# Another written-out order for a one-core attention and gated projection kernel, with zero products in the early gaps, a first load in three pieces and a last block in two halves

## The chip, the cores and the metric

The kernel runs on one core of one Trainium2 chip. The time is the device time of one execution in microseconds (us); the profile's span is the part of a profiled execution that the instructions fill. Engines are named as in the profile: PE multiplies matrices (PEld is its weight load), DVE works on vectors, ACT evaluates functions, POOL is hardly used, SP issues most loads. SPq and ACTq are the queues from which DMAs are issued.

## The reference, cut to what matters

Eight batches, eight heads, 512 local and 32 global positions, head dimension 64. Global queries see all 544 keys; a local query sees the 32 global keys and the local keys at most 32 positions away.

```python
s_g = scale * np.matmul(q_g, k_all.transpose(0, 1, 3, 2))
out_g = np.matmul(sm(s_g), v_all)
mask = np.abs(pos[:, None] - pos[None, :]) <= window        # window = 32
s_ll = np.where(mask, scale * np.matmul(q_l, k_l.transpose(0, 1, 3, 2)), -1e9)
out_l = np.matmul(sm(np.concatenate([s_lg, s_ll], axis=-1)), np.concatenate([v_g, v_l], axis=2))
x = concatenate([out_g, out_l], axis=2)  ->  (B, 544, 512)
gate = sigmoid(causal convolution of x along the positions, 5 taps, one weight per channel)
out = (gate * (x @ w_val)) @ w_out
```

## The kernel before, in words

A **unit** u is two heads of one batch; there are 32, four to a batch b. One unit's local attention is a chain of tasks, each of which is a few instructions on one engine:

- s{u} (PE, L567): 32 small score products in a program row, 64 in the trace, 64x32 weights each;
- mx{u}.h (DVE, L579): adds the mask, scales, and takes the maximum, four instructions per half h with one read of the accumulator behind each;
- exp{u}.h (ACT, L586), t{u}.h (PE transposes, L592), tc{u}.h (a copy out of PSUM, ACT L404 or DVE L406);
- av{u} (PE, L603): 64 value products in the trace; den, rec (DVE); norm{u} (DVE, one instruction, or ACT, eight, L624); xt{u} (PE transposes, L632); xc{u} (copy).
- Then xh, xl split the result into two parts for the wide products, and tap, conv build the gate on DVE. For the first two units the convolution is done on PE (pc, L693) with diagonal matrices that ACT makes (dg, L682).

The global queries of a batch have their own chain (gs, gmax, gexp, gt, gtc, gav, gden, grec, gnorm, gx, gxc). The two weights arrive as 64-bit numbers and are turned into a high and a low 32-bit part on DVE and ACT (w{k}.s0 to s7 and w{k}.high). For each batch then follow g1 (PE, L717: three products of 512 columns for each of 16 pairs of tiles), the gate (gv, gh, gl), and g2 (PE, L739: the same for the output weight), a copy ob and a store st. The 256 global rows of all batches are done last under the key "g" (gxh, gxl, gconv, sigg, g1.g, g2.g, ob.g, st.g; tiles ghg, glg, obg).

**What sets the order.** A long string `ORDER` names every task once, in one line, with the engine where there is a choice ("tc1.0:DVE") and the PSUM bank ("s4@53"). Every engine gets its instructions in the order in which its tasks stand in that string. A planner (`Plan.order`) walks it, keeps count of buffers and banks, and estimates times; the estimates set no waits, but decide where `keep_clock` puts products of zeros (L803) into PE's line: in before wherever the estimated gap is over `KEEP` = 900 ns, up to the first g1. Loads on SP are issued in the order of the string and wait for the PE instruction that stands ahead of them there. The first 13 loads are issued at once: q0, mask, q1, w0, q2, v0, q3, w1, v1, w2, v2, w3, v3 (L416, L953), q{u} being queries and keys of a unit, v{u} its values.

The last store: ACT copies the first half of obg (L745), DVE copies the second half (L746), then four DMAs of 64 KB write it, two from SP and two from ACT (L939).

Of the kernel before, what the change touches and what calls it, by code (L numbers as in the profile page):

```python
# [19 lines left out]
KW = 5  # L20
# [30 lines left out]
cw s0@01 mx0.0 mx0.1 exp0.0 w0.s0 s1@23 mx1.0 exp0.1 exp1.0 w0.s1 t0.1@1 t0.0@0 mx1.1 exp1.1 tc0.0 w0.s2 w0.s3 tc0.1 dg0  # L51
w0.s4 t1.0@2 w0.s5 t1.1@3 w0.s6 tc1.0:DVE av0@0 w0.s7 den0 rec0 norm0 s2@24 mx2.0 xt0@5 w0.high dg1 xc0 w1.s0 gs0@06
halo0 pc0.0@5 w1.s1 exp2.0 t2.0@2 tc1.1 mx2.1 w1.s2 gmax0.0 pc0.1 xh0 w1.s3 gmax0.1 w1.s4 w2.s0 pc0.2 w1.s5 exp2.1 tc2.0
av1@6 w2.s1 den1 w1.s6 rec1 w2.s2 w1.high iq4 xl0 t2.1@4 gexp0.1 s3@23 gexp0.0 tc2.1 w2.s3 norm1:ACT gt0.0@0 w1.s7
gtc0.0 mx3.0 pc0.3 w2.high w3.s0:ACT xt1@4 mx3.1 pc0.4 xc1 w3.s1 wi4 w2.s4 av2@0 w3.s2 gav0.0@4 exp3.1 halo1 den2 w3.s3
gt0.1@2 exp3.0 gtc0.1 w2.s5 conv0.3 w3.s4 pc1.0@6 t3.1@7 w2.s6 t3.0@2 xh1 iq5 w3.s5 iq6 rec2 norm2:ACT gav0.1 tc3.0 iv4
w3.s6 w2.s7 iq7 w3.s7 xl1 tc3.1 s4@53 xt2@0 w4.s0:ACT gden0 mx4.0 pc1.1 grec0 w4.s1 gnorm0 w4.s2 mx4.1 pc1.2 gx0@7 w4.s3
xc2 av3@4 exp4.0 gxc0 fix0 den3 s5@73 exp4.1 w4.s4 t4.0@2 tap2:ACT xh2 t4.1@0 iv5 pc1.3 rec3 halo2:ACT mx5.0 pc1.4 xl2
tc4.0 g1.0.0.0@7 norm3:ACT tc4.1 conv2.0 w4.s5 conv2.1 xt3@2 av4@0 conv1.3 w4.s6 exp5.0 xc3 w4.high conv2.2 w4.s7 t5.0@6
g1.0.0.1 den4 tc5.0 conv2.3 xh3 g1.0.0.2 rec4 s6@62 tap3:ACT mx5.1 norm4 exp5.1 wi5 xl3 w3.high gs1@40 t5.1@3 mx6.0  # L60
g1.0.0.3 exp6.0 halo3:ACT tc5.1 mx6.1 xt4@6 gmax1.0 fix1 exp6.1 gexp1.0 wi6 iv7 conv3.0 t6.0@2 w5.s0:ACT av5@4
g1.0.1.0@3 gmax1.1 den5 conv3.1 g1.0.1.1 g1.0.1.2 xc4 iv6 tc6.0 g1.0.1.3 t6.1@2 rec5 g1.0.2.0@6 gexp1.1 g1.0.2.1 w5.s1
conv3.2 w5.s2 conv3.3 w6.s0:ACT w5.s3 sig0 w6.s1 w5.s4 w5.high g1.0.2.2 norm5 s7@01 w5.s5 sig1 gv.0.0 tc6.1 w6.s2 w5.s6
gv.0.1 gt1.0@4 iq8 w5.s7 sig2 gh.0.0 g1.0.2.3 mx7.0 gtc1.0 gl.0.0 wi7 iq9 g1.0.3.0@7 gh.0.1 g1.0.3.1 sig3 iq10 g1.0.3.2
av6@4 w6.s3 exp7.0 gav1.0@0 gv.0.2 den6 gt1.1@2 gtc1.1 mx7.1 rec6 w6.s4 gl.0.1 xt5@6 exp7.1 g1.0.3.3 g2.0.0.0@1 norm6
gv.0.3 w7.s0:ACT t7.0@4 tc7.0 t7.1@5 w6.s5 tc7.1 gav1.1 w7.s1 gh.0.2 av7@2 iv8 w6.s6 w7.s2 w6.s7 gden1 gl.0.2 gh.0.3
iq11 w7.s3 w6.high den7 xc5 xt6@5 g2.0.0.1 iv10 grec1 g2.0.0.2 w7.s4 rec7 w7.s5 xh5 norm7:ACT gnorm1 s8@46 iv9 s9@70
# [123 lines left out]
class Plan:  # L191
# [38 lines left out]
    def order(self):  # L230
# [8 lines left out]
        def put(t):  # L239
# [12 lines left out]
            if t.eng != "FREE":  # L252
                at = max(at, free[t.eng])
# [48 lines left out]
            if t.eng == "DMA" and t.name != "first":  # L302
                self.loads = self.loads[-15:] + [(max([t.start + BEGINS] + [b for _, b in self.loads[-1:]]), t.end + LANDS)]
# [731 lines left out]
```

## Time and profile before

| | us |
|---|---|
| median of 3 runs | 362.09 |
| the three runs | 360.68, 362.09, 363.57 |
| the profiled execution | 361.64 |
| its span | 359.9 |
| PE busy | 349.9 |
| DVE busy | 315.3 |
| ACT busy | 254.3 |

PE is busy nearly throughout: of the 40 equal slices of the span every one but the last is at 8 tenths or more, and most at 9 or more. ACT is at 9 tenths for most of the first quarter and falls off later. A matmul's end is modelled, and consecutive matmuls overlap in the record, so PE's pace is read from start to start. The granted PE clock is below 9 tenths of full speed in one slice only, the second, which runs from 9 to 18 us.

### The profile page before, as it was taken

The page shows a single profiled execution, that of the slowest core. Times are in us where ns is not written, and L with a number is a line of the kernel's source. Part 1 is how long each engine was busy: PE and PEld are TensorE (multiplying, and loading weights), DVE is VectorE, ACT ScalarE, POOL GpSimd, SP SyncE. Part 2 cuts the span into 40 slices and gives each one's busy share as a digit, 9 for nine tenths or more (in the row PEclk, how much of TensorE's full clock was granted, in tenths as well). Part 3 has the DMA queues.
Part 4 walks back from the last instruction along what each step waited for, and adds up shares of the span by engine and source line. Part 5 has one row for each costly group of instructions (what it writes and reads, how often), then busy time and mean ns, then how long its engine had stood idle before and what let it go on. Part 6 is the DMA issues. An engine that isn't in the chain of part 4 may idle for free.

```text
span 359.9 us, 14810 instructions
## 1 busy us (share of the span) xinstructions
PE 349.9 (97%) x6331; PEld 280.0 (78%) x6331; DVE 315.3 (88%) x1085; ACT 254.3 (71%) x652; POOL 0.8 (0%) x7
## 2 busy tenths in 40 slices
PE   8899999899999999999999999999999999999995
PEld 4666687778787888788878877888878888888894
DVE  4899999999989899899899997989599696988981
ACT  3899999897897688987788566776659458523131
POOL 0000000000000000000000000000000000000000
PEclk9899999999999999999999999999999999999999
DMA  7995947695675734925666482823854101000223
GB/s 280 400 362 166 359 156 279 209 402 193 226 235 199 276 104 108 391 102 171 221 241 237 159 277 104 262 67 132 283 165 173 62 2 51 13 29 36 112 87 87
DMA packets 17249, 66.73 MB, mean 185 GB/s; under 512 B 1952, under 2 KB 4000, under 8 KB 17184
## 3 DMA queue, kind: packets, MB, share of 16 engines
q1 hardware_dynamic: 12240, 57.12, 45.2%
q10 hardware_dynamic: 4944, 8.67, 6.6%
q8 instruction: 49, 0.80, 0.9%
q14 instruction: 16, 0.13, 0.1%
HBM read 56.87 MB, written 8.91 MB: 183 GB/s over the span
## 4 chain that ended last, share of the span: by engine, by line
PE 81%; ACT 8%; DMA 5%; DVE 3%; issue 1%; SPq 1%; ACTq 0%; DVEq 0%
PE psum L717 25%; PE psum L739 23%; PE psum L603 7%; PE psum L567 7%; PE psum L592 7%; PE psum L632 4%; DMA v<-in_vw_dram 3%; PE psum L531 3%; DMA out_dram<-ob 2%; ACT pm L586 2%; PE psum L493 2%; ACT xs L624 2%; PE psum L511 1%; DVE gate L668 1%; ACT xc L404 1%
## 5 line engine op out<-in xcount | busy, mean ns | idle before, releaser
L586 ACT ACTIVATE pm<-pm,mx 128x128 f32<-128x128 f32 x256 | 80.9, 407 | 25.8 <-DVE mx L579 22.5
L668 DVE SCALAR_TENSOR_TENSOR gate<-xc,cw,gate 128x512 f32<-128x512 f32 x120 | 87.7, 745 | 1.1 <-ACT gate L397 0.4
L579 DVE CUSTOM_DVE_ANT_0 pm<-psum,mask 128x128 f32<-128x128 f32 x256 | 57.4, 285 | 5.2 <-PE psum L567 5.2
L717 PE MATMUL psum<-xh,wvh 128*128 128x512 f32 x128 | 53.8, 421 | 0.0
L739 PE MATMUL psum<-woh,gh 128*128 128x512 f32 x128 | 53.0, 414 | 0.0
L717 PE MATMUL psum<-xl,wvh 128*128 128x512 f32 x128 | 50.6, 396 | 0.0
L717 PE MATMUL psum<-xh,wvl 128*128 128x512 f32 x128 | 50.5, 395 | 0.0
L739 PE MATMUL psum<-woh,gl 128*128 128x512 f32 x128 | 50.2, 392 | 0.0
L739 PE MATMUL psum<-wol,gh 128*128 128x512 f32 x128 | 50.0, 391 | 0.0
L404 ACT COPY pts<-psum 128x512 f32<-128x512 f32 x49 | 28.6, 601 | 16.0 <-PE psum L592 16.0
L592 PE MATMUL psum<-ident,pm 128*128 128x128 f32 x256 | 38.0, 278 | 0.6 <-ACT pm L586 0.3
L567 PE MATMUL psum<-qk 64*32 64x128 f32 x2048 | 38.1, 281 | 0.5 <-ACT pm L586 0.4
L603 PEld LDWEIGHTS psum<-v,pts 128*32 128x32 f32 x2048 | 31.1, 111 | 8.3 <-issue 4.7
L567 PEld LDWEIGHTS psum<-qk 64*32 64x32 f32 x2048 | 30.3, 108 | 8.5 <-issue 3.6
L592 PEld LDWEIGHTS psum<-ident,pm 128*128 128x128 f32 x256 | 29.6, 140 | 9.1 <-ACT pm L586 2.7
L603 PE MATMUL psum<-v,pts 128*32 128x65 f32 x2048 | 34.9, 224 | 1.4 <-DMA v<-in_vw_dram 1.2
L717 PEld LDWEIGHTS psum<-xh,wvl 128*128 128x128 f32 x128 | 24.0, 188 | 5.6 <-issue 0.2
L739 PEld LDWEIGHTS psum<-woh,gl 128*128 128x128 f32 x128 | 24.0, 188 | 5.3
L717 PEld LDWEIGHTS psum<-xh,wvh 128*128 128x128 f32 x128 | 24.3, 190 | 4.5 <-DVE xl L664 0.2
L717 PEld LDWEIGHTS psum<-xl,wvh 128*128 128x128 f32 x128 | 24.2, 189 | 4.1 <-issue 0.2
L739 PEld LDWEIGHTS psum<-woh,gh 128*128 128x128 f32 x128 | 24.2, 189 | 4.0 <-issue 0.2
L739 PEld LDWEIGHTS psum<-wol,gh 128*128 128x128 f32 x128 | 24.2, 189 | 3.9
(111 smaller groups left out, 554.0 us busy)
## 6 DMA issues: line engine op xcount, KB each, us to landing
v<-in_vw_dram SPq DMA_DIRECT2D x32, 975.0 KB, 6.7
qk<-in_qk_dram SPq DMA_DIRECT2D x32, 624.0 KB, 5.0
out_dram<-ob ACTq DMA_DIRECT2D x32, 256.0 KB, 2.2
wraw<-in_w_val_dram SPq DMA_DIRECT2D x4, 512.0 KB, 12.3
wraw<-in_w_out_dram SPq DMA_DIRECT2D x4, 512.0 KB, 4.1
mask<-in_mask_dram SPq DMA_DIRECT2D x1, 256.0 KB, 4.6
out_dram<-obg SPq DMA_DIRECT2D x4, 64.0 KB, 1.7
out_dram<-obg ACTq DMA_DIRECT2D x4, 64.0 KB, 2.0
```

The lines of the kernel that those rows point to most:

```text
L404: A.copy(out, in_)
L493: on_pe(T.matmul(s[h][SG * c:SG * c + SG, cols], qkt[rows, SL + SG * h:SL + SG * h + SG], keys, start=True, stop=True))
L531: on_pe(T.matmul(ag[SG * c:SG * c + SG, :], pgt[:k, s, SG * c:SG * c + SG], vt[:k, w, h, :], start=(n == 0), stop=(n == len(steps) - 1)))
L567: on_pe(T.matmul((sx, sy)[h][32 * j:32 * j + 32, i, :], qkt[rows, 32 * m:32 * m + 32], qkt[rows, k0:k0 + P], start=True, stop=True))
L579: V.tensor_tensor_reduce(out=pm[:, h, i, :], in0=s[:, i, :], in1=mask[:, i, :], op0=ALU.add, op1=ALU.min, scale=-SCALE, scalar=3.0e38, acc ...
L586: A.activation(out=pm[:, h, i, :], in_=pm[:, h, i, :], func=AF.Exp, bias=mx[:, c:c + 1], scale=-1.0)
L592: on_pe(T.transpose(pt[:, i, :], pm[:, h, i, :], ident))
L603: on_pe(T.matmul(ax[32 * j:32 * j + 32, h, E1 * i:E1 * i + E1], pts[:, h, i, 32 * j:32 * j + 32], vt[:, block_win(4 * i + j), h, :], start ...
L632: on_pe(T.transpose(xt[:, P * i:P * i + P], xs[:, i].rearrange("p h d -> p (h d)"), ident))
L668: V.scalar_tensor_tensor(out=acc, in0=xc[:, k:k + SL], scalar=cw[:, u % NDT, k:k + 1], in1=acc, op0=ALU.mult, op1=ALU.add)
L717: on_pe(T.matmul(box["pv", e], w[:, e, t * P:t * P + P], x, start=(t == 0 and q == 0), stop=(t == NDT - 1 and q == 2)))
L739: on_pe(T.matmul(box["po", r], g[:, e, rs], w[:, e, :], start=(e == 0 and q == 0), stop=(e == NDT - 1 and q == 2)))
```

## The change

The string ORDER is replaced by another one over the same tasks. What is done, and how often, stays the same but for the points below; the sequence on every engine, the engine of some copies, and the banks are new. Around it:

- the constants of the planner change (what a block of PE's instructions counts, what a load counts), and the rule for zeros: now every estimated gap over 350 ns up to 15 us, at most 8 products each;
- the first load is cut in three by columns (640, 320 and 288 of 1248). For that the query columns stand on both sides of the keys in memory (`q_col`); the first piece holds what the first half of s0 reads;
- the mask is loaded from ACT's queue, behind craw, and no longer from SP's, behind q0;
- the two products of zeros at the very start read a constant instead of the cleared tile zf, 432 columns instead of 512;
- the last block of rows, g2.g.1, is computed as two halves of 256 columns into two banks; the first half is copied by DVE and stored while the second is computed, and the second is copied by ACT alone. Each half is one DMA from SP, and the block before it one DMA from ACT, instead of four DMAs from both;
- the global rows lie in xgT with the batch innermost, so that the convolution of the global rows reads adjacent elements; its steps alternate between two tiles.

```diff
-KEEP = 900
+KEEP, EARLIER, MOST = 350, 15000, 8
...
-        transfer(t, qk[u])
+        for a, b in zip((EARLY[0], 0, EARLY[1]), (EARLY[1], EARLY[0], QK)) if u == 0 else ((0, QK),):
+            transfer(t[:, a:b], qk[u, :, a:b])
...
+        def g2_halves(r, e):
...
+            c, rs = e * 2 // NDT, slice(r * P, r * P + P)
+            for k in range(e * 2 % NDT, e * 2 % NDT + 2):
+                for q, (g, w) in enumerate(((box["gh"], woh), (box["gh"], wol), (box["gl"], woh))):
+                    on_pe(T.matmul(box["half", c][:, :DM // 2], g[:, k, rs], w[:, k, c * DM // 2:(c + 1) * DM // 2],
+                             start=(k == 0 and q == 0), stop=(k == NDT - 1 and q == 2)))
+            if (c, k) == (0, NDT - 1):
+                o = sb.tile([P, DM // 2], F32, tag="gv", name="obg_first")
+                V.tensor_copy(o, box["half", 0][:, :DM // 2])
+                store(r, o, 0)
...
-            if (key, r) == ("g", n // P - 1):
-                A.copy(box["ob", r][:, :DM // 2], box["po", r][:, :DM // 2])
-                V.tensor_copy(box["ob", r][:, DM // 2:], box["po", r][:, DM // 2:])
+            if last_part:
+                A.copy(o, box["half", 1][:, :DM // 2])
...
+    def conv_pair(n):
+        if n not in paired:
+            paired.add(n)
+            for k in range(KW):
+                for dt in (2 * n, 2 * n + 1):
+                    gp[dt][2](k)
...
-        for s in range(P // SG):
-            (A if s % 2 else nc.sync).dma_start(out[r * (P // SG) + s, 0:SG, :], o[s * SG:s * SG + SG, :])
+        cols = slice(0, DM) if r == 0 else slice(c * DM // 2, (c + 1) * DM // 2)
+        (nc.sync if r else A).dma_start(out[:, P // B * r:P // B * r + P // B, cols].rearrange("b q d -> q b d"), o)
...
+        A.dma_start(mask, maskd)
...
-        keep_clock(2, 7, zf)
+        keep_clock(2, 7, nc.const_aps.tensor_like(0.0, zf[:, :WARM]))
...
-                if not opened and gap > KEEP:
-                    keep_clock(int((gap - 400) * 0.55 / 235), t.spare)
+                if t.start < EARLIER and gap > KEEP:
+                    keep_clock(min(int((gap - 150) / 240), MOST), t.spare)
```

**What moves.** On PE, at the start of the program, the sequence before was as follows (qk_81, qk_84, qk_88 are the loads of units 0, 1, 2; pm_155 and pm_205 the probabilities of units 0 and 1; v_90 the values of unit 0; zr and zf are zeros):

```order
L803 MATMUL psum<-zf 128x512 x2
L567 MATMUL psum<-qk_81 32x128 x32
L803 MATMUL psum<-zr 128x512
L567 MATMUL psum<-qk_84 32x128 x32
L592 MATMUL psum<-ident,pm_155 128x128 x8
L592 MATMUL psum<-ident,pm_205 128x128 x8
L803 MATMUL psum<-zr 128x512 x2
L603 MATMUL psum<-v_90,pts_157 32x65 x32
```

The same place on PE after the change (qk_82, qk_86, qk_90 are units 0, 1, 2; pm_157 and pm_218 units 0 and 1; v_92 the values of unit 0):

```order
L834 MATMUL psum<-const-float32-0.0 128x432 x2
L579 MATMUL psum<-qk_82 32x128 x32
L834 MATMUL psum<-zr 128x512 x5
L579 MATMUL psum<-qk_86 32x128 x32
L834 MATMUL psum<-zr 128x512 x8
L604 MATMUL psum<-ident,pm_157 128x128 x4
L604 MATMUL psum<-ident,pm_218 128x128 x4
L604 MATMUL psum<-ident,pm_157 128x128 x4
L834 MATMUL psum<-zr 128x512 x2
L615 MATMUL psum<-v_92,pts_159 32x65 x32
L604 MATMUL psum<-ident,pm_218 128x128 x4
```

There are 15 products of zeros (zr) between the first score products and the first value products, where there were 3, and half of unit 1's transposes now stand behind av0.

On ACT at the same place, before (diag_241 to diag_346 are the diagonal matrices of dg0 and dg1):

```order
L959 ACTIVATE table<-zf 128x1
L586 ACTIVATE pm_155<-pm_155,mx_156 128x128 x8
L586 ACTIVATE pm_205<-pm_205,mx_206 128x128 x8
L404 COPY pts_157<-psum 128x512 x2
L682 ACTIVATE diag_241<-ident,cw 128x128 x4
L682 ACTIVATE diag_246<-ident,cw 128x128
```

and after:

```order
L1000 ACTIVATE table<-zf 128x1
L694 ACTIVATE diag_170<-ident,cw 128x128 x4
L694 ACTIVATE diag_175<-ident,cw 128x128
L598 ACTIVATE pm_157<-pm_157,mx_158 128x128 x4
L598 ACTIVATE pm_218<-pm_218,mx_219 128x128 x4
L598 ACTIVATE pm_157<-pm_157,mx_158 128x128 x4
L415 COPY pts_159<-psum 128x512
```

The five instructions of dg0 now stand ahead of the first exponentials, which wait for the maxima; they stood behind them.

At the end of ACT's sequence, before (obg_5952 is the first block of global rows, obg_5964 the last):

```order
L404 COPY obg_5952<-psum 128x512
L939 DMA out_dram<-obg_5952 32x512 x2
L745 COPY obg_5964<-psum 128x256
L939 DMA out_dram<-obg_5964 32x512 x2
L1030 UNCONDITIONAL_BRANCH
```

and after:

```order
L415 COPY ob_0_5936<-psum 128x512
L950 DMA out_dram<-ob_0_5936 128x512
L415 COPY obg_5961<-psum 128x512
L981 DMA out_dram<-obg_5961 16x8x512
L776 COPY obg_5976<-psum 128x256
L1071 UNCONDITIONAL_BRANCH
```

The last copy of ACT is followed by no DMA on ACT any more; that store is issued on SP.

More of the change, by code (lines that the diff above doesn't have):

```diff
@@ L50 @@
 ORDER = """
[L51 to L55, printed above, removed]
@@ L146 @@
-gh.g.2:DVE ob.6.3 gl.g.2 g1.g.3.3 st.6.3 g2.g.0.0@4 gv.g.3 gh.g.3:DVE g2.g.0.1 ob.7.3 g2.g.0.2 gl.g.3 g2.g.0.3
-g2.g.1.0@5 st.7.3 g2.g.1.1 ob.g.0 g2.g.1.2 st.g.0 g2.g.1.3 ob.g.1 st.g.1
+cw s0@01 mx0.0 mx0.1 w0.s0 dg0 exp0.1 s1@23 mx1.0 exp1.0 w0.s1 exp0.0 t0.0@2 tc0.0 mx1.1 w0.s2 t1.0@3 w0.s3 t0.1@1 tc1.0
+exp1.1 w0.s4 tc0.1:DVE av0@2 w0.s5 t1.1@1 dg1 w0.s6 s2@04 den0 w0.high:DVE rec0 w1.s0:ACT tc1.1 w0.s7 norm0 gs0@62 mx2.0
+mx2.1 exp2.0 xt0@0 w1.s1 gmax0.0 xc0 w1.s2 halo0 pc0.0@0 exp2.1 av1@6 w1.s3 w2.s0:ACT gmax0.1 s3@12 w1.s4 w2.s1 w1.s5
@@ L282, in put @@
                     else:
[L283 to L284 removed]
+                        x = sent - BEGINS
+                        here = sent + IDLE + max(0, min(AHEAD_OF, max([b - x for a, b in self.loads if a <= x] + [0])))
                         if free["DMA"] > sent:
@@ L302, in put @@
             if t.eng == "DMA" and t.name != "first":
-                self.loads = self.loads[-15:] + [(max([t.start + BEGINS] + [b for _, b in self.loads[-1:]]), t.end + LANDS)]
+                self.loads = self.loads[-15:] + [(due, t.end)]
             line.append(t)
@@ L732, in gl @@
                             op=ALU.subtract)
+        def g2_halves(r, e):
+            if e % (NDT // 2) == 0:
+                used = [plan.at[f"g2.{key}.{i}"][0] for i in (r - 1, r)]
+                spare = next(n for n in (f"g1.{key}.{i}" for i in range(NDT)) if plan.at[n][0] not in used)
+                box["half", e * 2 // NDT] = bank(spare if e else f"g2.{key}.{r}")
+            c, rs = e * 2 // NDT, slice(r * P, r * P + P)
[7 more added lines that the diff above has]
+                store(r, o, 0)
         def g2(r, e):
+            if (key, r) == ("g", n // P - 1):
+                g2_halves(r, e)
+                return
             if e == 0:
@@ L878, in attention_moe @@
         plan.add(f"rec{u}", "DVE", 118, lambda u=u: l_rec(u), [f"den{u}"])
-        plan.add(f"norm{u}", (("DVE", 608), ("ACT", 1320)), 0, lambda u=u: l_norm(u), [f"rec{u}"], take=[("xs", u)],
+        plan.add(f"norm{u}", (("DVE", 608), ("ACT", 1585)), 0, lambda u=u: l_norm(u), [f"rec{u}"], take=[("xs", u)],
                  give=[("pair", f"av{u}")])
```

263 lines of the change are left out of this document (137 added, 126 removed).

## The prediction

> **What bounds the kernel now.** I read the page's busy shares first, then the table of busy time by stretches, on both sides of s8, the first score product of the third batch. That is a fair milestone: the same PE tasks stand ahead of it in both lines. It starts at 71.94 us.
>
> ```profile
> PE 349.9 (97%) x6331; PEld 280.0 (78%) x6331; DVE 315.3 (88%) x1085; ACT 254.3 (71%) x652; POOL 0.8 (0%) x7
> ...
> 71.94:355.74 283.80, 282.51 (x4886) 232.09 (x4886) 251.52 (x825) 191.06 (x481) 0.00 (x0) 1.00 0.47 164
> 5.16:71.94 66.78, 63.69 (x1450) 46.78 (x1456) 62.41 (x257) 61.40 (x169) 0.00 (x0) 0.97 0.78 283
> ```
>
> The columns are the stretch and its length, then busy time of PE, PEld, DVE, ACT, POOL, the granted clock, the DMA share and GB/s. Behind s8 PE is the bound: idle for 283.80 - 282.51 = 1.29 us. Ahead of s8 three engines are nearly full at once: PE is idle for 3.09 us, DVE for 66.78 - 62.41 = 4.37, ACT for 66.78 - 61.40 = 5.38. So the whole that a better order can win in waits is 3.09 + 1.29 = 4.38 us of PE's time, beside slow clock, start and end. Next, the timeline of PE in the head (start, duration, work, count, and the idle time before it with what ended it):
>
> ```profile
> 5.16 1.96 PE L567 MATMUL psum<-qk 64*32 64x128 f32 x64
> ...
> 7.73 1.16 PE L567 MATMUL psum<-qk 64*32 64x128 f32 x64
> 9.23 3.50 PE L592 MATMUL psum<-ident,pm 128*128 128x128 f32 x16 [0.34 <-ACT pm L586]
> 12.49 0.71 PE L803 MATMUL psum<-zr 128*128 128x512 f32 x2
> 14.44 1.96 PE L603 MATMUL psum<-v,pts 128*32 128x65 f32 x64 [1.24 <-DMA v<-in_vw_dram]
> 16.33 1.81 PE L567 MATMUL psum<-qk 64*32 64x128 f32 x64
> ...
> 23.13 1.12 PE L603 MATMUL psum<-v,pts 128*32 128x65 f32 x64
> 24.18 0.65 PE L592 MATMUL psum<-ident,pm 128*128 128x128 f32 x4
> 24.77 1.16 PE L567 MATMUL psum<-qk 64*32 64x128 f32 x64
> ```
>
> The value products of unit 0 wait for their load until 14.44. They and the score products behind them then take 1.96 and 1.81 us, where the same groups take 1.12 and 1.16 later. The clock says why; the windows are cut where it changes:
>
> ```profile
> 11.05:14.46 3.41, 2.17 (x11) 0.99 (x13) 3.27 (x10) 3.41 (x12) 0.00 (x0) 1.00 1.00 385
> 14.46:17.87 3.41, 3.41 (x127) 3.20 (x128) 1.88 (x5) 2.30 (x8) 0.00 (x0) 0.50 1.04 401
> ```
>
> PE was busy for 2.17 of 3.41 us, and the next 3.41 us ran at half clock. DMA is full all through (385 to 401 GB/s). Last, the list of waits of PE (total, times, longest), and the timeline of the end:
>
> ```profile
> PE psum L603 <- DMA v<-in_vw_dram: 1.2, 1, 1.2
> PE psum L531 <- issue: 1.2, 1, 1.2
> PE psum L632 <- ACT ob L404: 0.5, 1, 0.5
> PE psum L567 <- ACT pm L586: 0.4, 1, 0.4
> ```
>
> ```profile
> 355.33 0.39 PE L739 MATMUL psum<-woh,glg 128*128 128x512 f32 x1
> 355.75 0.37 ACT L745 COPY obg<-psum 128x256 f32<-128x256 f32 x1 [2.13 <-PE psum L739]
> 356.16 0.42 DVE L746 COPY obg<-psum 128x256 f32<-128x256 f32 x1 [4.64 <-ACT obg L745]
> 356.61 0.78 SPq L939 DMA_DIRECT2D out_dram<-obg  x2
> 356.62 0.85 ACTq L939 DMA_DIRECT2D out_dram<-obg  x2
> ```
>
> The two copies of the last block run one behind the other, then two DMAs on each queue.
>
> **The change part by part.** The sum is made against the profiled execution, 361.64 us: a span of 359.9 and 1.74 around it, which nothing here touches.
>
> **The end.** The prices of wide products, from the chain of waits, and of stores, from the list of DMA issues (KB each, us to landing):
>
> ```profile
> 333.70 10.88 PE psum L739 x48
> 344.58 5.69 PE psum L717 x48
> ...
> out_dram<-ob ACTq DMA_DIRECT2D x32, 256.0 KB, 2.2
> ...
> out_dram<-obg SPq DMA_DIRECT2D x4, 64.0 KB, 1.7
> out_dram<-obg ACTq DMA_DIRECT2D x4, 64.0 KB, 2.0
> ```
>
> A 512-column product takes 10.88 / 48 = 0.227 us, a 256-column one 5.69 / 48 = 0.119. The last block's 12 of the first kind become 24 of the second: 24 x 0.119 - 12 x 0.227 = +0.13. Behind it, only ACT's copy of 0.37 stands between PE's end at 355.73 and the store, which SP issues at about 356.15. Before, the later of ACT's two DMAs was issued at 356.62 + 0.85 / 2 = 357.04. That is 0.89 less. The landing took 1.7 from SP and 2.0 from ACT for 64 KB; 256 KB took 2.2. The new last store of 128 KB in rows of 1 KB lies between: I take 1.95, so -0.05, with ends of -0.3 and +0.2. Together -0.8 (ends -1.1 and -0.55). The first half's copy and store lie under the second half's 12 products (1.4 us); were they not covered, SP would issue the last store up to 0.4 later.
>
> **The zeros and the clock.** Half clock cost 1.96 - 1.12 = 0.84 on the value products and 1.81 - 1.16 = 0.65 on the scores: 1.5 us. In the new line 15 zero products stand where there were 3, all in stretches in which PE waits for loads or exponentials. I take half, -0.7, because ACT and DVE are nearly as full as PE up to s8 and part of the gain ends in a wait for them. The ends are -1.5 and +0.5 (zeros that run at half speed and hold up a transpose). The page "TensorE: Matmul & The Clock Gate" of the Trainium skill (What's actually happening) says that the clock falls after an idle window of about 3.4 us; by that the term would be 0 with or without zeros, since no gap here is that long. The trace disagrees: the window before the half clock was busy for 2.17 of its 3.41 us.
>
> **The first load in pieces, the mask on ACT's queue, dg0 first.**
>
> ```profile
> 0.73 0.39 SPq L416 DMA_DIRECT2D qk<-in_qk_dram  x1
> ...
> 5.33 0.18 DVE L366 TENSOR_SCALAR cva<-craw 128x20 int32<-128x20 int32 x1 [3.48 <-DMA craw<-in_convT_dram]
> ...
> 7.22 0.29 DVE L579 CUSTOM_DVE_ANT_0 pm<-psum,mask 128x128 f32<-128x128 f32 x1 [0.43 <-PE psum L567]
> ...
> 7.56 4.79 ACT L586 ACTIVATE pm<-pm,mx 128x128 f32<-128x128 f32 x16 [4.89 <-DVE mx L579]
> 12.26 1.05 ACT L404 COPY pts<-psum 128x512 f32<-128x512 f32 x2
> 13.20 1.57 ACT L682 ACTIVATE diag<-ident,cw 128x128 f32<-128x128 f32 x5
> ```
>
> Two more issues on SP at 0.39 stand ahead of q1, one fewer for the mask: later loads are issued some 0.4 us later, but at 385 to 401 GB/s their bytes queue anyway, so 0. s0 can begin on the first piece. What that frees is bounded by the 0.43 for which DVE waited for s0, because ahead of that DVE waits for craw, whose load is not moved: -0.2 (ends -0.43 and +0.4). Putting dg0 (1.57) ahead of the exponentials uses ACT's 4.89 us wait: ACT starts on dg0 when DVE is done with the taps (seven steps of some 0.21 from 5.33, so 6.8), and is then 7.56 - 6.8 = 0.76 ahead in volume. The first transpose, at 9.23, moves to 6.8 + 1.57 + 3 x 1.2 = 12.0 (4.79 / 4 = 1.2 for four exponentials); with 1.05 for two copies and 0.3 for the transposes, unit 0's probabilities are ready at 13.4, still ahead of the load that av0 needs (14.4). Cost 0; without that cover it would be up to 2.8.
>
> **The order itself.** PE has four kinds of work: scores, values, transposes and wide products. In PE's whole sequence one kind gives way to another 230 times before and 247 times after. What a change costs, from the chain of waits:
>
> ```profile
> 57.34 1.09 PE psum L567 x64
> ...
> 71.94 1.96 PE psum L567 x128
> ```
>
> Two score groups apart cost 2 x 1.09 = 2.18, side by side 1.96: 0.22 for one excursion, that is 0.11 for a change. 17 x 0.11 = 1.9 at most; many of the added changes lead from transposes to wide products, where none of these rows shows a loss. I take +1.0 (ends 0 and +1.9). Against this stand PE's waits. The 1.2 for v0 stays, since that load is not earlier. The 1.2 under "issue", the 0.5 and the 0.4 belong to places of the old line and go with it; the new line will have some of its own, for which there is no row. Of 4.38 us of idle time I take -1.2 (ends -3.5 and +2).
>
> The interleaved convolution of the global rows lies beside PE, whose pieces at 333.70 and 344.58 above join without a gap: 0.
>
> Sum: -0.8 - 0.7 - 0.2 + 1.0 - 1.2 = -1.9, so 361.64 - 1.9 = 359.7 for a profiled execution. The median of the three runs is 0.45 above the profiled one; of that I add half and predict **359.9**.
>
> **The rivals.** **A fuller head (faster).** If the new order lets PE run through to s8, it wins most of the 3.09 and the 1.5 of half clock, say 3.7, and all 1.29 behind s8: 361.64 - 0.8 - 3.7 - 1.3 + 0.6 = 356.4. For it: both lines have the same PE work there, and DVE and ACT have 4.4 and 5.4 us to spare. Against it: loads set av0 and the units behind it.
>
> **DVE decides the head (slower).**
>
> ```profile
> L731 DVE TENSOR_TENSOR gl<-gv,gh 128x512 fp32r<-128x512 f32 x32 | 21.6, 686 | 0.4 <-ACT gh L404 0.2
> ...
> L406 DVE CAST gh<-gv 128x512 fp32r<-128x512 f32 x12 | 4.9, 410 | 0.1
> ```
>
> In the new line four DVE tasks at 0.69 (tc0.1, norm1, gl.0.3, w7.s7) and four at 0.41 (w0.high, w4.s0, gh.0.0, w7.s6) come to stand ahead of s8, and two of each (tc1.0, norm4; w1.s0, w2.s0) leave: 2 x 0.69 + 2 x 0.41 = +2.2 on an engine with 4.37 idle. If PE's chains to s8 wait for that, s8 comes 2.2 later, the clock wins nothing, and 361.64 - 0.8 + 2.2 + 1.0 = 364.0. It decides if s8 starts after 73 with DVE idle for under 2.5 us before it.
>
> **The places change nothing.**
>
> ```profile
> 68.75 0.11 PEld L531 LDWEIGHTS psum<-v,pgt 128*32 128x32 f32 x2 [1.33 <-issue]
> ...
> q8 instruction: 49, 0.80, 0.9%
> ```
>
> PE's instructions arrive in 49 transfers (2 x 6331 / 49 = 258 each), and one late block costs 1.33. Where such a wait falls may depend on how long a block takes in full DMA queues, and not on the line. Then the waits come back elsewhere, the -1.2 is 0, and the result 361.64 - 0.8 - 0.7 - 0.2 + 1.0 = 360.9. The page "Runtime: NRT & Kernel Launch" of the Trainium skill (Instruction fetch mechanics) has blocks of 256 instructions too, with a cost that is mostly hidden; the 1.33 us here was not.
>
> **How the numbers follow.** Chances: forecast 0.43, fuller head 0.27, DVE 0.13, places 0.17. One per cent, about what a measurement tells from no change, is 3.6 us: faster is below 358.5, slower above 365.7. Faster is most of the fuller head (0.24) and a seventh of the forecast (0.06): 0.30. Slower is a third of the DVE case with its waits at their upper end (0.05). The range, 356.0 to 363.8, holds the forecast with its ends, the places and the middle of both others; it leaves out the far half of each, some 0.2.
>
> **What would show it.** In the new profile: clock 1.00 in the stretch around 14.46 to 17.87 and value products of unit 0 at 1.1 us; s8 starting between 70 and 72 (forecast), below 69 (fuller head), above 73 (DVE); PE idle behind s8 below 1.3; from PE's last product to the end of the span 3.3 us, where it was 4.1. The prediction fails if waits under "issue" are over 3 us on PE, or if s8 moves by more than 3 us either way.

## The result, and the profile after

The changed kernel takes 363.68 us, the median of 16 executions (361.71 to 366.56), against 362.55 of the kernel before beside it: a ratio of 1.005 with a 95% interval of 1.0028 to 1.0073. Ratios here and below leave out executions over 1.5 per cent above the fastest of their kernel, and are not quotients of the medians (that would be 1.0031). It is slower by some half a per cent: 1.1 us by the medians, 1.8 by the ratio. The time lies inside the predicted range, at its slow end (363.8), but the prediction of 359.9 pointed the other way: its sum of -1.9 stands against +1.1. The profiled execution took 363.04, 1.40 more than the one before.

The busy times of the changed kernel by stretches (the stretch and its length, then busy time of PE, PEld, DVE, ACT, POOL, granted clock, DMA share, GB/s) are cut at s8, which starts at 73.33, and at PE's end:

```profile
0.00:73.33 73.33, 68.58 (x1458) 48.78 (x1458) 64.13 (x260) 63.46 (x171) 0.85 (x7) 1.00 0.77 271
73.33:357.53 284.20, 284.09 (x4899) 231.48 (x4898) 248.45 (x822) 194.63 (x475) 0.00 (x0) 1.00 0.46 164
```

The same two stretches of the kernel before, now cut at its first s8 product at 71.87:

```profile
0.00:71.87 71.87, 67.33 (x1446) 47.89 (x1446) 63.26 (x260) 62.82 (x171) 0.85 (x7) 0.98 0.77 276
71.87:355.72 283.85, 282.58 (x4887) 232.16 (x4886) 251.59 (x825) 191.13 (x481) 0.00 (x0) 1.00 0.47 164
```

s8 comes 1.46 later. Behind it PE's idle time falls from 283.85 - 282.58 = 1.27 to 284.20 - 284.09 = 0.11, but its busy time grows by 1.51, so the stretch is 0.35 longer. Behind PE's end the span is 0.5 shorter (below). These three make 1.3 of the 1.40. The timeline of PE in the head of the changed kernel (start, duration, work, count, and the idle time before it with what ended it) shows where s8's delay begins:

```profile
0.77 3.22 PE L834 MATMUL psum<-const-float32-0.0 128*128 128x432 f32 x4 [0.77 <-PEq L1062]
3.92 1.11 PE L579 MATMUL psum<-qk 64*32 64x128 f32 x32
5.94 1.11 PE L579 MATMUL psum<-qk 64*32 64x128 f32 x32 [0.91 <-DMA qk<-in_qk_dram]
6.98 2.50 PE L834 MATMUL psum<-zr 128*128 128x512 f32 x5
9.41 1.28 PE L579 MATMUL psum<-qk 64*32 64x128 f32 x64
10.62 2.14 PE L834 MATMUL psum<-zr 128*128 128x512 f32 x8
12.75 2.04 PE L604 MATMUL psum<-ident,pm 128*128 128x128 f32 x12
14.54 0.71 PE L834 MATMUL psum<-zr 128*128 128x512 f32 x2
15.18 1.14 PE L615 MATMUL psum<-v,pts 128*32 128x65 f32 x64
16.26 0.66 PE L604 MATMUL psum<-ident,pm 128*128 128x128 f32 x4
16.84 1.16 PE L579 MATMUL psum<-qk 64*32 64x128 f32 x64
...
21.44 1.10 PE L705 MATMUL psum<-xc,diag 128*128 128x512 f32 x2 [1.39 <-DVE xc L653]
...
57.59 1.11 PE L615 MATMUL psum<-v,pts 128*32 128x65 f32 x64 [0.97 <-DVE wraw L391]
```

The first half of s0 runs 1.24 earlier than s0 did, but the second half waits 0.91 for the last piece. The five zeros behind it take 0.5 each, where the eight later ones take 0.27, and s1 starts at 9.41 (7.73 before). av0 starts at 15.18 (14.44 before) and no longer waits for its load. Its products take 1.14, not 1.96: the half clock is gone from this place. Still, PE spent 8.57 us of busy time on zeros up to there (3.22 + 2.50 + 2.14 + 0.71). In the kernel before it was 3.78 in the warm-up,

```profile
1.45 3.78 PE L803 MATMUL psum<-zf 128*128 128x512 f32 x4 [1.45 <-DVE zero L955]
```

and 0.75 and 0.71 in the two rows that the prediction shows: 5.24. Ahead of s8, PE was idle for 73.33 - 68.58 = 4.75 us, where it was 71.87 - 67.33 = 4.54. Two waits for DVE, 1.39 and 0.97, are new; the waits for v0's load (1.24) and under issue (1.2) are gone. ACT's timeline shows what s1's delay does:

```profile
8.32 1.28 ACT L598 ACTIVATE pm<-pm,mx 128x128 f32<-128x128 f32 x4 [1.09 <-DVE mx L591]
11.08 2.45 ACT L598 ACTIVATE pm<-pm,mx 128x128 f32<-128x128 f32 x8 [1.48 <-DVE mx L591]
```

After four exponentials of unit 0 come four of unit 1, which wait 1.48 for the maxima of s1; the other four of unit 0, which av0 needs, stand behind them.

The end, as PE's last product, ACT's copy and SP's store in the timeline, and the store's row in the list of DMA issues (KB, us to landing):

```profile
357.25 0.28 PE L754 MATMUL psum<-woh,glg 128*128 128x256 f32 x1
357.57 0.37 ACT L776 COPY obg<-psum 128x256 f32<-128x256 f32 x1 [2.28 <-PE psum L754]
357.97 0.55 SPq L981 DMA_DIRECT2D out_dram<-obg  x1
```

```profile
out_dram<-obg SPq DMA_DIRECT2D x1, 128.0 KB, 2.3
```

From PE's end (357.53) to the end of the span (361.1) are 3.6 us, where they were 4.1. The copy and the issue are where the prediction put them; the store lands after 2.3 and not 1.95.

### The profile page after: what moved, and what is told of

It reads as the page before. It is cut to its first block, busy times and chain, and to the rows that moved or that the text cites. A ratio compares the mean times of both kernels' runs of the same rounds, so it can differ in the third digit from the quotient of the medians.

```text
span 361.1 us, 14854 instructions
## 1 busy us (share of the span) xinstructions
PE 352.7 (98%) x6355; PEld 280.3 (78%) x6355; DVE 312.6 (87%) x1080; ACT 258.5 (72%) x645; POOL 0.8 (0%) x7
## 4 chain that ended last, share of the span: by engine, by line
PE 92%; DVE 3%; DMA 3%; issue 1%; SPq 0%; ACT 0%; DVEq 0%
PE psum L729 26%; PE psum L769 25%; PE psum L579 9%; PE psum L615 8%; PE psum L604 8%; PE psum L644 4%; DMA qk<-in_qk_dram 3%; PE psum L543 3%; PE psum L505 2%; PE psum L705 2%; PE psum L523 2%; PE psum L834 1%; PE psum L525 1%; PE psum L754 1%; DVE pg L512 1%
## 5 line engine op out<-in xcount | busy, mean ns | idle before, releaser
L598 ACT ACTIVATE pm<-pm,mx 128x128 f32<-128x128 f32 x256 | 80.5, 397 | 14.8 <-DVE mx L591 14.4
L769 PE MATMUL psum<-woh,gh 128*128 128x512 f32 x128 | 54.3, 424 | 0.0
L415 ACT COPY pts<-psum 128x512 f32<-128x512 f32 x53 | 30.3, 587 | 17.6 <-PE psum L604 17.5
L579 PE MATMUL psum<-qk 64*32 64x128 f32 x2048 | 37.3, 278 | 1.6 <-DMA qk<-in_qk_dram 1.6
L579 PEld LDWEIGHTS psum<-qk 64*32 64x32 f32 x2048 | 29.2, 107 | 10.1 <-issue 5.0
L737 DVE TENSOR_TENSOR gv<-psum,gate 128x512 f32<-128x512 f32 x32 | 21.8, 685 | 6.8 <-PE psum L729 6.0
```

The lines of the kernel that those rows point to most:

```text
L415: A.copy(out, in_)
L579: on_pe(T.matmul((sx, sy)[h][32 * j:32 * j + 32, i, :], qkt[rows, q_col(m):q_col(m) + 32], qkt[rows, k0:k0 + P], start=True, stop=True))
L598: A.activation(out=pm[:, h, i, :], in_=pm[:, h, i, :], func=AF.Exp, bias=mx[:, c:c + 1], scale=-1.0)
L737: V.tensor_tensor(out=box["gv", e], in0=box["pv", e], in1=gates[x0 + e], op=ALU.mult)
L769: on_pe(T.matmul(box["po", r], g[:, e, rs], w[:, e, :], start=(e == 0 and q == 0), stop=(e == NDT - 1 and q == 2)))
```

## The experiments

Each ratio is to the kernel before, run beside it, with its 95% interval. What each theory says stands in the expectation ahead of the result; what a profile shows is one execution of that kernel.

### The start: zeros and the gap in s0

**Two zeros more in the gap of s0.**

```diff
         for i in range(4):
+            if (u, i) == (0, 2):
+                keep_clock(2, 2, nc.const_aps.tensor_like(0.0, zf[:, :WARM]))
             for n in range(8):
```

> The changed kernel with two more zero products (432 columns) between the two halves of s0, where its PE stood idle for 0.91 us. In the changed kernel the score products ran at half speed until 9.7 us and the five zeros behind s0 took 2.50 us, so that s1 began at 9.41 although its load had landed at 7.79. Clock theory (the idle 0.91 us kept the clock down for one more window of 3.41 us): full speed from some 6.3 us, the five zeros take 1.2 us, s1 begins at 8.2, av0 at 13.9 instead of 15.2, and the time falls by 1.2 to 362.5 us. Zeros theory (the five zeros hold up s1 at any clock): s1 at 8.2 or later, a gain of at most 0.5. Line theory (the new line is late in its own right, by its order of exponentials and by pc0.0 behind VectorE): no change, 363.7.

1.0021 (0.9993 to 1.005). The head did what the clock theory says: s1 at 8.59, av0 at 14.29, s8 at 72.26, 1.07 earlier than in the changed kernel. Behind s8 the profile took all of it back. The timeline of PE there:

```profile
126.42 0.39 PE L771 MATMUL psum<-woh,gh 128*128 128x512 f32 x1
127.77 0.50 PE L771 MATMUL psum<-wol,gh 128*128 128x512 f32 x1 [0.96 <-issue]
```

Two products of one row, 0.23 apart elsewhere, stand 1.35 apart, with no engine and no load to wait for. The changed kernel's profile has no such wait in that stretch. That the filled gap brought the clock up is not shown by this profile alone: the trace's record of the granted clock has full speed from 4.90 us here, but from 5.25 in the third profile of the changed kernel itself, where the gap is not filled (below).

**No zeros between s0 and s1.**

```diff
-                if t.start < EARLIER and gap > KEEP:
+                if t.start < EARLIER and gap > KEEP and t.name not in ('s1',):
```

> The changed kernel without the five zero products between s0 and s1; all other zeros stay. Zeros theory: s1 begins at 7.8 instead of 9.4, ends by 9.8 even at half speed instead of 10.6, exp1.0 starts 0.9 to 1.6 earlier, and the time falls by 0.8 to 1.5, to 362.2 to 362.9 us. Clock theory: the window in which the zeros kept PE busy is then not full, the clock comes up a window later (about 13 us), s1, the next zeros and the transposes run at half speed, and the time is within 0.4 of 363.7 or above it. Line theory: 363.7.

1.0057 (1.0023 to 1.0092): no gain, so the zeros theory falls in its simple form. PE's timeline:

```profile
8.29 1.71 PE L579 MATMUL psum<-qk 64*32 64x128 f32 x64 [2.00 <-DMA qk<-in_qk_dram]
9.93 3.09 PE L834 MATMUL psum<-zr 128*128 128x512 f32 x8
```

q1 itself came at 8.3 in this execution, and half clock followed (1.71 for products that take 1.16; eight zeros in 3.09). All of its executions had a mean clock of 0.995 or less, as 5 of the 38 of the changed kernel in the ratios had; one stretch of 3.41 us at half clock takes 3.41 / 2 / 361 = 0.005 off the mean. So the five zeros do keep the clock up. What they cost by holding up s1 and what they gain by the clock come out nearly even: 1.0057 without them, 1.0050 with them.

### The new code with the old line, and the reverse

**The old line in the new code, with the new rule for zeros.** The string ORDER of the kernel before is put into the changed kernel; the planner then puts fourteen zeros behind s0, eleven more than in the kernel before.

> The code of the changed kernel (load in pieces, mask on ScalarE's queue, zeros in early gaps, split last block) with the line of the kernel before: 5 zeros ahead of s1, 1, 1 and 2 ahead of transposes and 5 ahead of av0. Line theory (the loss is in the new line): 362.5 of the kernel before, less 0.45 for the end and up to 1.5 for the clock: 360.6 to 362.0. Clock and zeros theory (the loss is in the code of the start): s1 at 9.4 here too; ScalarE has eight exponentials of unit 0 to do meanwhile, so av0 comes at 14.4 to 15.2, and the time is 362 to 363.3.

1.0207 (1.016 to 1.0254, from four executions), which no theory had. s8 was in time (72.07). Behind it PE's timeline has this:

```profile
93.84 0.27 PE L644 MATMUL psum<-ident,xs 128*128 128x128 f32 x1 [3.08 <-issue]
...
94.93 0.63 PE L729 MATMUL psum<-xh,wvh 128*128 128x512 f32 x1
```

A wait of 3.08 us under issue, in the middle of one task of four transposes; behind it the products run at half clock (0.63 instead of 0.39; the granted clock is 0.50 from 94.29 to 97.70). All waits of PE under issue come to 6.4 us in this profile, and to 1.2 in the kernel before.

**The new line in the old code.** The reverse.

> The code of the kernel before with the new line alone: one load for q0, few zeros, last block whole. Line theory: the loss of the new line stands alone and without the end's gain, 363.7 + 0.45 = 364.2 or more. Clock and zeros theory: s1 at 7.7 as in the kernel before, exp1.0 not held up, and the time is that of the kernel before within 0.5: 362.0 to 363.0.

1.0023 (0.9991 to 1.0055), between the two theories. The head was good (s8 at 71.25). Its profile has one new long wait late in the program, where the old code's global convolution, in one piece, fills DVE ahead of a copy that PE needs:

```profile
342.28 0.50 PE L739 MATMUL psum<-woh,gh 128*128 128x512 f32 x1 [1.04 <-DVE ob L406]
```

### Which part of the start

**The whole old start**, with the new line and the new end: q0 in one load, mask on SP's queue, old rule for zeros.

```diff
-        for a, b in zip((EARLY[0], 0, EARLY[1]), (EARLY[1], EARLY[0], QK)) if u == 0 else ((0, QK),):
-            transfer(t[:, a:b], qk[u, :, a:b])
+        transfer(t, qk[u])
...
-        A.dma_start(mask, maskd)
...
+            elif kind_ == "mask":
+                nc.sync.dma_start(mask, maskd)
...
-                if t.start < EARLIER and gap > KEEP:
-                    keep_clock(min(int((gap - 150) / 240), MOST), t.spare)
+                opened = opened or bool(t.take and t.take[0][1].startswith("g1."))
+                if not opened and gap > 900:
+                    keep_clock(int((gap - 400) * 0.55 / 235), t.spare)
```

> The changed kernel with the start of the kernel before: q0 in one load, mask behind it on SyncE's queue, and the earlier rule for zeros (only in planned gaps over 0.9 us, 2 instead of 5 ahead of s1, none ahead of av0). New line, split last block and interleaved global convolution stay. The new line alone ran 0.2 per cent above the kernel before, with a wait of 1.04 us for VectorE at 342 and without the split end. Start theory (the loss lies in the load in pieces and the zeros): that figure less 1.0 for the wait and 0.45 for the end: 0.2 per cent below the kernel before or better, 361.0 to 361.7 us, and s8 starts by 72. Line theory (the loss lies in the new order): within 0.5 of the changed kernel, 363.2 or more.

1.0012 (0.9981 to 1.0044), s8 at 71.80. Better than the changed kernel, as the start theory says, but not below the kernel before.

**One load for q0, new zeros** (that diff without its last piece).

> The changed kernel with q0 in one load and the mask behind it on SyncE's queue; the new zeros stay. If the load in pieces is the cause (PE stands idle for 0.9 us within s0, and q0's last piece lands at 5.8 instead of 5.1): s0 runs in one piece from 5.1, s1 starts by 8.6, and the time falls by 1 or more, to 362.7 or less. If the five zeros ahead of s1 are the cause: s1 still starts at 9 or later in most executions, and the time stays within 0.5 of 363.7.

1.0017 (0.9983 to 1.0051). s1 at 7.59 and av2 at 28.49, 1.5 ahead of the changed kernel; but s8 at 73.14, because PE stood still for 1.70 between two products of s6:

```profile
46.29 1.06 PE L578 MATMUL psum<-qk 64*32 64x128 f32 x51
49.05 0.44 PE L578 MATMUL psum<-qk 64*32 64x128 f32 x13 [1.70 <-issue]
```

**Old zeros, load in pieces** (its last piece alone).

> The changed kernel with the earlier rule for zeros alone (2 ahead of s1, 6 ahead of the first transposes, none ahead of av0, 2 ahead of the first convolution product); q0 stays in pieces. If the zeros are the cause: s1 starts by 8.3 and the time is 362.7 or less. If the load in pieces is the cause: within 0.5 of 363.7. If the early zeros earn their time by the clock, as the prediction had it: above 364.

1.0033 (0.9999 to 1.0068), s8 at 73.65: not told from the changed kernel.

**Two of the five zeros moved into the gap of s0.**

```diff
         for i in range(4):
+            if (u, i) == (0, 2):
+                keep_clock(2, 2)
...
-                    keep_clock(min(int((gap - 150) / 240), MOST), t.spare)
+                    keep_clock(3 if t.name == 's1' else min(int((gap - 150) / 240), MOST), t.spare)
```

> The changed kernel with two of the five zeros behind s0 put between the two halves of s0, so that PE has no idle time there and the number of instructions is the same everywhere behind s1. With four short zeros in that place s8 came 1.07 us earlier, but PE then waited 1.34 us under issue at 126.4, where the changed kernel has no such wait. Clock theory: s8 starts by 72.3 in the profile (73.3 in the changed kernel), no wait under issue of 1 us behind it, and the time falls by 1.0 or more to 362.7 or less. Instruction theory (a wait of that kind is as likely at any number of instructions): a wait over 0.8 us under issue shows again somewhere, and the time is 363.2 or more.

1.0024 (0.9994 to 1.0053). The profile is as the clock theory has it: s8 at 72.00, and no wait of 0.8 under issue behind it. The time lies between the two expectations.

Each of the last four undoes a part of the start and comes out 0.15 to 0.4 per cent better than the changed kernel, with intervals that overlap. No part stands out.

### The old line with its own number of instructions

**The kernel before with the new end and the interleaved convolution alone.** In the code of the changed kernel with the old ORDER, q0 and mask as above, and

```diff
-                if t.start < EARLIER and gap > KEEP:
-                    keep_clock(min(int((gap - 150) / 240), MOST), t.spare)
+                if t.name in {'s1': 1, 'av0': 2}:
+                    keep_clock({'s1': 1, 'av0': 2}[t.name], t.spare)
```

> The kernel before with the split last block, its whole-row stores and the interleaved global convolution alone: old line, q0 in one load, mask on SyncE's queue, one zero ahead of s1 and two ahead of av0 as before; PE's sequence is that of the kernel before up to the last block. What the end is worth by itself: in the changed kernel's profile PE's last product is 3.6 us from the end of the span instead of 4.1, and the split costs 0.13 on PE, so 0.4 less, 0.1 per cent below the kernel before: 361.6 to 362.3. If the end gained what the prediction gave it (0.8): 361.3 to 361.9. If the interleaved convolution holds up the old line's end: 362.5 or more.

1.0005 (0.9976 to 1.0034): the end gains nothing that can be measured. (The warm-up's zeros are the new ones here too.)

**The same with the load in pieces and the mask on ACT's queue.**

> The code of the changed kernel, its load in pieces and mask on ScalarE's queue included, with the old line and the old zeros (one ahead of s1, two ahead of av0), so that PE's sequence is that of the kernel before up to the last block. The same with eleven more zeros ahead of av0 ran 2.1 per cent above the kernel before; there PE waited 3.08 us under issue at 93.8 and 1.33 at 118.5. Instruction theory (the eleven zeros moved the ends of the instruction blocks to bad places): those two waits are gone and the time is within 0.8 of the kernel before, 361.7 to 363.2. Code theory (something else in the new code does not agree with the old line): 365 or more.

0.9974 (0.9944 to 1.0005). Against the 1.0207 above, eleven zero products are all that differs; PE's waits under issue are 2.1 us in this profile, where they were 6.4. That agrees with the instruction theory, but the eleven also stood in places where they can hold work up; a run below takes that away.

**The changed kernel again.**

> The changed kernel, beside the others of this set on the same chip: 0.5 per cent above the kernel before again (0.2 to 0.8), 363.2 to 364.8, if the difference belongs to the kernel; nearer to 0 if it came from where the clock's windows lay in the earlier runs.

1.0044 (1.0013 to 1.0076). Its profile has, in s6, what the first had not:

```profile
50.41 0.45 PE L579 MATMUL psum<-qk 64*32 64x128 f32 x14 [1.83 <-issue]
```

and s8 at 75.31.

**One load for q0, again.**

> The changed kernel with q0 in one load and the mask behind it on SyncE's queue, again, beside the changed kernel itself on the same chip. If the load in pieces costs the 1.2 us that the first comparison points to: 0.2 to 0.5 per cent below the changed kernel. If it costs nothing: within 0.15 per cent of it.

1.0035 (1.0013 to 1.0057), 0.1 per cent from the changed kernel beside it: the gain of the first set is not confirmed. It too stood still in s6 (1.82 under issue, ahead of 50.04).

### The number of instructions by itself

**Ten more products in the warm-up, new line.** The warm-up keeps its length, since the zeros are narrower (each product of a constant runs as two passes):

```diff
-        keep_clock(2, 7, nc.const_aps.tensor_like(0.0, zf[:, :WARM]))
+        keep_clock(7, 7, nc.const_aps.tensor_like(0.0, zf[:, :P]))
```

> The changed kernel with seven zero products of 128 columns in the warm-up instead of two of 432 (each runs as two passes, so 14 rows instead of 4, of the same total length): all that stands behind is ten products further on in the instruction stream, and nothing else differs. Instruction theory: the wait of 2.0 us under issue at 47 to 50 is gone from the profile, waits of that kind may come elsewhere; the time differs from the changed kernel's by more than 0.3 per cent, downwards (362 to 363) if no new wait comes. Start theory (the loss is in the load in pieces and the zeros, which are the same): 363.4 to 364.8 as before.

1.0204 (1.0139 to 1.027, from five executions). Head as before (av0 at 14.54), then, in PE's timeline,

```profile
27.86 4.32 PE L705 MATMUL psum<-xc,diag 128*128 128x512 f32 x6 [1.95 <-issue]
```

and half clock behind it: six convolution products take 4.32, where eight took 3.60. The wait in s6 is gone, as expected; but the time is up and not down. PE's waits under issue come to 4.8 us in this profile; in the three of the changed kernel they are 0, 1.8 and 0.6.

**The same in the old line with the new end.**

> The old line with the new end (0.05 per cent above the kernel before), with the same ten more products in the warm-up at the same length of it. Instruction theory: this alone makes waits under issue of 1 us and more behind 20 us, as eleven more zeros did, and the time is 365 to 370. If those 2 per cent came from where the eleven zeros stood (ahead of s1, the transposes and av0): 361.6 to 363.0.

1.0205 (1.015 to 1.0261, from five executions), against 1.0005 without them. PE's list of waits under issue (total, times, longest) begins with these; all come to 6.6 us, and to 1.2 without the ten:

```profile
PE psum L728 <- issue: 3.6, 2, 2.7
PE psum L578 <- issue: 1.3, 2, 1.0
PE psum L542 <- issue: 1.1, 1, 1.1
```

So ten more products of zeros, in time in which PE has nothing else to do, cost 1.6 per cent (5.6 us) in the new line and 2.0 (7.2 us) in the old, most of it in waits under issue. Not every other number does this: with five fewer (no zeros ahead of s1) or four more (the gap of s0 filled) the new line's waits under issue were 0.2 and 1.0 us, and the times 1.0057 and 1.0021.

**The old line with the load in pieces, again.**

> The new code, load in pieces included, with the old line and the old zeros, again: 0.26 per cent below the kernel before in the first set, with an interval that just touches 0. If that holds: 361.0 to 362.2, faster than both kernels. If not: 362.0 to 363.0.

1.0015 (0.9979 to 1.0051): not faster than the kernel before.

**The changed kernel a third time.**

> The changed kernel a third time, for one more profile and more times: 0.4 to 0.5 per cent above the kernel before, 363.4 to 364.6. Instruction theory: the profile shows a wait of 1.9 to 2.1 us under issue between 46 and 51 (likely, three in four so far), and s8 starts later than 74.5 if it does. Start theory: no such wait and s8 at 73.3.

1.0049 (1.0016 to 1.0081). Its profile shows no wait of 1.9 in s6, and s8 at 73.22, though the head had full clock early:

```profile
6.16 1.43 PE L834 MATMUL psum<-zr 128*128 128x512 f32 x5
8.25 1.16 PE L579 MATMUL psum<-qk 64*32 64x128 f32 x64 [0.66 <-DMA qk<-in_qk_dram]
...
57.45 0.77 PE L615 MATMUL psum<-v,pts 128*32 128x65 f32 x39 [1.13 <-DVE wraw L391]
```

Five zeros took 1.43 here and 2.50 in the first profile, av2 came 0.65 earlier (29.39 against 30.04), and of that 0.11 is left at s8. The wait for DVE, 1.13 at av5, took up some of it.

### DVE's and ACT's order in the new head

**halo0 and xc0 first.** `xt0@0 w1.s1 gmax0.0 xc0 w1.s2 halo0 pc0.0@0` becomes `xt0@0 xc0 halo0 w1.s1 gmax0.0 w1.s2 pc0.0@0`, with the zeros held at 5, 8 and 2.

> The changed kernel with two tasks of the line moved: xc0 (ScalarE's copy) and halo0 (VectorE's clearing of four columns, 0.06 us) stand right behind xt0, ahead of w1.s1, gmax0.0 and w1.s2; TensorE's sequence and the zeros are the same. Line theory: the wait of 1.39 us of the first convolution product falls to 0.7 or less, av2 and s8 come 0.7 earlier than in the changed kernel (av2 29.3, s8 72.5 where s8 was 73.2 to 73.3 without a wait under issue), and the time falls by 0.2 per cent, to 0.3 per cent above the kernel before. If VectorE or a load is the bound behind it: av2 comes earlier but av5 still at 57.5, s8 at 73.2, and the time stays at 0.5 per cent above.

1.0076 (1.0044 to 1.0108). The wait of the first convolution product falls as expected, to 0.68, and now ends with ACT's copy:

```profile
21.18 1.13 PE L607 MATMUL psum<-xc,diag 128*128 128x512 f32 x2 [0.68 <-ACT xc L317]
```

The time does not fall: av2 at 30.29, s8 at 74.31.

**And exp0.0 ahead of exp1.0, with the zeros moved.** In addition `exp0.1 s1@23 mx1.0 exp1.0 w0.s1 exp0.0` becomes `exp0.1 exp0.0 s1@23 mx1.0 w0.s1 exp1.0`; two zeros between the halves of s0, 3 ahead of s1, 6 ahead of the transposes, 4 ahead of av0.

> The same, and exp0.0 ahead of exp1.0 on ScalarE, and the fifteen zeros in other places: two between the halves of s0, three ahead of s1, six ahead of the first transposes, four ahead of av0; the number of TensorE's instructions is that of the changed kernel behind av0. Start theory: ScalarE no longer waits for s1, av0 comes at 13.5 to 14 instead of 15.2, av2 at 28.0 to 28.5, s8 at 71.5 to 72, and the time falls by 0.4 to 0.6 per cent in all, to within 0.1 per cent of the kernel before. If the bound lies behind av2 (loads, VectorE): s8 at 73 and 0.4 per cent above.

1.0054 (1.0027 to 1.0081). av0 at 14.25 and s8 at 72.61 are earlier, about half as much as expected. Behind s8, PE's 285.25 us hold 0.97 of idle time where the changed kernel has 0.11:

```profile
72.61:357.86 285.25, 284.28 (x4899) 231.41 (x4898) 248.53 (x821) 194.52 (x475) 0.00 (x0) 1.00 0.46 163
```

The theory that these two places make the new line slow falls: mended, they gain no time. Why the first of the two runs is above the changed kernel (1.0076) is not shown.

### What the runs say together

| line | start | ratios | mean |
|---|---|---|---|
| new | new | 1.0050, 1.0044, 1.0049 | 1.0048 |
| new | pieces, old zeros | 1.0033 | 1.0033 |
| new | one load, new zeros | 1.0017, 1.0035 | 1.0026 |
| new | one load, old zeros | 1.0012 | 1.0012 |
| old | pieces, old zeros | 0.9974, 1.0015 | 0.9995 |
| old | one load, old zeros | 1.0005 | 1.0005 |

All have the new end. The three sets in the first row against the three in the last two differ by 0.5 per cent, with a 95% uncertainty of some 0.25: 1.8 us, give or take 0.9. That the loss belongs to the new line together with the new start is therefore shown. How it divides between them is not: each step down the table is within its uncertainty. The profiles point further than the times. s8 starts at 73.33, 75.31 and 73.22 in the changed kernel, at 71.80 in the new line with the whole old start, and at 71.03, 71.72 and 72.75 in the old line with the new end; so its delay goes with the start, as far as single profiles tell. Behind s8, PE is busy for 284.0 to 284.3 us in the new line with either start, and for 282.2 to 282.8 in the old line.

## Why the prediction was wrong

**The end (-0.8, ends -1.1 and -0.55).** Mis-sized. The span behind PE's end shrank from 4.1 to 3.6, and the split costs the 0.13 on PE that was worked out: -0.4, outside the ends. The term that failed is the landing, 2.3 us for 128 KB and not 1.95. By itself, with the old line, the end gave 1.0005.

**The zeros and the clock (-0.7, ends -1.5 and +0.5).** The half clock of av0 and s2 went, as predicted: 0.82 + 0.65 = 1.5. Another came: the record of the granted clock has full speed from 7.63 us in the profile before and from 9.70 after it, and s0 and s1 took 0.26 + 0.12 longer. Net 1.1. PE's busy time ahead of s8 without the zeros fell by 2.1 (67.33 - 5.24 = 62.1 to 68.58 - 8.57 = 60.0); 0.8 of that is the first sixteen transposes (3.50 before, 2.04 + 0.66 after), which ran at full clock both times. And the price was read from one execution. Of 133 executions of the kernel before beside the experiments, 20 had a mean clock of 0.995 or less, as the profiled one (0.994) had; their mean is 362.8 us, against 362.1 for the others. The difference of 0.7 is uncertain by 0.8; in the five other kernels of this case with three or more executions of both kinds it lies between -0.6 and +1.7, with a mean of 1.0. So what there was to win was some 0.7 to 1.0 in one execution out of seven: 0.1 on average, 0.15 at most by these means.

**The first load (-0.2, ends -0.43 and +0.4).** DVE's first maximum came at 7.14 and not 7.22: s0's early half helps nobody, since the second half waits for a piece that lands later than the whole load did. ACT's first exponential came at 8.32 (7.56 before), because the half of unit 0 that the new line puts first needs all eight maxima. "Cost 0" for dg0 and the exponentials rested on v0's load as a cover until 14.4. The cover was not enough: av0 started at 15.18 with no wait for its load. The prediction had named a cost in that case of up to 2.8; 0.74 came.

**The order, changes of kind (+1.0, ends 0 and +1.9).** The best of the terms. PE's busy time behind s8 grew by 1.51, of which 0.13 is the end: +1.4. All 17 added changes of kind lie behind s8 (175 there before, 192 after), which makes 0.08 for each, where 0.11 was worked out. That the changes are the cause is argued from this, since no run varies their number alone; that the growth is a property of the line is shown. The same stretch in the first repeat of the changed kernel, and in the old line with the new end:

```profile
75.31:359.60 284.29, 284.17 (x4899) 231.61 (x4898) 248.49 (x822) 194.62 (x475) 0.00 (x0) 1.00 0.47 164
```

```profile
71.03:354.02 282.99, 282.31 (x4899) 233.07 (x4898) 251.60 (x829) 191.69 (x485) 0.00 (x0) 1.00 0.47 165
```

**PE's waits (-1.2, ends -3.5 and +2).** This is the step that failed. Behind s8 it held: -1.16, down to 0.11 of idle time. Ahead of s8 the prediction counted the waits that go with the old line and, having no row for the new one's, gave it hardly any. It has more: zeros and idle time together are 8.57 + 4.75 = 13.3 us in place of 5.24 + 4.54 = 9.8. The step "15 zero products ... all in stretches in which PE waits" is what hid it, since those stretches are longer in the new line: they were counted as places for zeros and not as a cost. s8's delay is the sum of the two: 3.5 more of these, less the 2.1 of other busy time above: about 1.4.

**The interleaved convolution (0).** Right for this line only because the code came with it: without it PE waited 1.04 at 342.28.

**The rivals.** The fuller head fell; s8 came later, not earlier. DVE decides the head (364.0) came near in number: s8 after 73, two new waits for DVE of 1.39 + 0.97 = 2.4 us where +2.2 was worked out. But its own condition, DVE idle under 2.5 ahead of s8, is not met: from 5.16 to s8 DVE is busy for 62.32 of 68.17 us, idle for 5.85. It would be met only from about av0 to av5: 42.76 - 41.42 = 1.34 in

```profile
14.83:57.59 42.76, 39.70 (x909) 27.63 (x908) 41.42 (x166) 41.03 (x116) 0.00 (x0) 1.00 0.77 274
```

where ACT is as full (1.73 idle). Moving one of DVE's tasks away freed the product that waited for it and gained no time; that the head is bound by both engines here is argued from this row, not shown. The places change nothing (360.9) had the mechanism that the later runs show most plainly, waits of PE for its own instructions, and priced it at 1.2, for waits that come back wherever they are moved. The changed kernel's profile has none, so they are not what made it slower there; ten more products bring 4.8 us of them, or 6.6 in the old line.

**What stays open.** How the 0.5 per cent divides between the new line, the load in pieces and the zeros, beyond what single profiles say; and why PE's instructions come late at some numbers and not at others. In s6 of the new line a wait of 1.8 us under issue came in the first repeat and in both profiles with one load, but not in the first and the third of the changed kernel, so that even at one number it is a matter of the single execution.

## What to carry to other kernels

Where one engine is busy for 97 per cent of the span, the number of instructions ahead of a point can be part of its tuning: an edit that adds instructions, even idle ones, is tested against a twin that has the same number at another place, or its cost is not the edit's. A rare event in the one profile at hand, such as a stretch of half clock, is priced by how often executions have it before it enters a sum. And a gap that is filled with zeros is still a gap: count zeros and idle time together when two orders are compared.

## What the runs showed of the hardware that was not expected

Ten products of zeros in the warm-up, twenty of PE's instruction slots where a transfer brings about 258, moved the time by +1.6 and +2.0 per cent in two different orders (1.0204 and 1.0205 against 1.0048 and 1.0005). Single waits under issue reached 3.1 us, and one of 1.95 was followed by half clock. The records of PE's instruction transfers (queue q8, 16 KB each) in the traces bear the reading out. The twenty profiles of this case hold 18 waits of PE under issue of 0.7 us or more behind 14 us; at each of them the last transfer had landed 1.1 to 1.7 us before the wait ended, though the 49 or 50 transfers of a profile are some 7 us apart. At the longest, from 90.76 to 93.84, it ran from 91.49 to 92.42: it began only after PE stood still. What sets the moment is not shown. The page "Runtime: NRT & Kernel Launch" of the Trainium skill (Instruction fetch mechanics) calls the cost of crossing a block mostly hidden; here the 0, 1.8 and 0.6 us of such waits in three profiles of the changed kernel are near that, and the 4.8 and 6.6 with ten more products are not.

The clock's windows lie elsewhere in each execution: the record of the granted clock has full speed from 9.70, 10.23 and 5.25 us in three profiles of the changed kernel, and within a record the changes lie multiples of 3.41 apart. In the first two, s0's second half still ran at half clock behind gaps of 0.91 and 0.80; in the third full clock came ahead of a gap of 0.51. Whether the gap within s0 delays the clock is therefore in part a matter of where the windows fall. The page "TensorE: Matmul & The Clock Gate" of the Trainium skill (What's actually happening) says that the window runs free and does not start with the kernel, and the trace agrees.
